# A mixture-of-experts kernel: the one-tile unit's second layer ahead of the next unit's transposes, and W1's low halves in two column halves

## The chip, the cores and the metric

The kernel runs on one core of a Trainium2 chip. The metric is the device time of one execution in microseconds. TensorE multiplies matrices, VectorE, ScalarE and GpSimd work elementwise, SyncE and GpSimd issue DMA transfers. Each engine runs its own instruction stream in order and waits for the others on semaphores.

## The reference

Attention with pooled keys and values, and then a routed two-layer network (8 experts) on the 4608 tokens that attention gives:

```python
k_p = k.reshape(B, H, Sp, 8, D).mean(axis=3); v_p = v.reshape(B, H, Sp, 8, D).mean(axis=3)
attn = softmax(scale * q @ k_p.T)                  # B = H = 8, 576 queries, 72 pooled keys, D = 64
x = (attn @ v_p).reshape(4608, 512)
do_compute = x @ w_skip > 0
xc = x[do_compute]
e_idx = argmax(xc @ w_gate);  gate_w = softmax(xc @ w_gate)[e_idx]
for e in range(8):                                 # w1[e]: 512 x 1024, w2[e]: 1024 x 512
    h = maximum(xc[e_idx == e] @ w1[e], 0.0)
    y[e_idx == e] = gate_w * (h @ w2[e])
out = x;  out[do_compute] = xc + y
```

All of it is float32. A product in the expert stage is made of three: each operand is split into a high half (rounded to the type that TensorE takes at full rate) and a low half (the rest), and high x high, low x high and high x low are added up in PSUM.

## The kernel before

**Stages.** The attention stage takes the first 150 us or so, writes x to the output and sorts the tokens by expert into a table. It also handles 256 tokens of the busiest expert ahead. What follows is the expert stage, `experts`, and the change lies there.

**Units.** Each expert's tokens are cut into tiles of 128. A unit is two tiles, an expert's last unit has three where the count of tiles is odd, and an expert with one tile has a unit of one. Places are 0, 1, 2: three tiles fill all, two fill 1 and 2, one fills 2 alone. The register `kind` says which it is: 0 is one tile, 1 two (`TWO` is 1), more than 1 three, and with three it also says how wide the first layer is, a step of `QUARTERS` by how full the last tile is. One and two tiles both run their first layer on columns 128 to 384. `ends` is 1 in an expert's last unit, 2 if its last tile has at most 64 tokens ("short"). `after` is the `ends` of the unit before. `left` counts the units still to come, this one with them.

**TensorE's order in a unit** (`unit` inside the tensor block): the first layer `first`, in eight blocks of 128 hidden columns `f`, 12 products each, with three PSUM tiles `psL` in turn. From `f` = 3 on it waits (`lo`) until VectorE is done with the block three before. Then `second(0)` and `second(1)` for the tiles in places 0 and 1, then `tx`, the transposes of the next unit's rows into `psD`, then the tile in place 2, as `second(2)` or, for a short tile, `second_short`. `tx` waits for `land0` to `land2`, which GpSimd gives once the gathered rows have landed. In a one-tile unit nothing stands between `first` and `tx`. `far_width` and `by_width` choose the body for the width with branches; TensorE's never had one for 352 and takes 384 there, ScalarE's and VectorE's did.

**ScalarE** makes the high half of each hidden block (`hhi`, ReLU). In an expert's first unit it makes the high halves of W2, one of four chunks at every second block; in an expert's last unit, behind the first layer, those of the next W1 (four chunks of 128 x 1024). Then it makes the high halves of the next x from `psD`, three tiles.

**VectorE** makes the low halves of the hidden blocks (`hlo`), of W2 and W1 (`split`), adds a second-layer result to its rows (`result`, `result_short`), and makes the low halves of x (`x_low`). Its order at the end of an expert is: four W1 splits, `result(0)` and `result(1)` where there are such tiles, `x_low` three times, which gives `x` and so lets TensorE's next `first` begin, then the result of place 2.

**Weight loads.** SyncE loads the weights in eight chunks of 512 KB an expert, strictly in order: four of W1, four of W2. A chunk's staging buffer is free once VectorE has split the chunk of the expert before (`wlo` counts the splits).

**GpSimd** scatters each finished tile to the output and gathers the rows of the unit after next into the freed ring buffer. It waits for a scatter's completion before it gathers into the same buffer, and only then for the landing of its gathers.

```python
with t.If(left > 1):
    tx(u)
with t.If(kind < TWO):
    for _ in range(3):
        P(t, "lo")
P(t, "psf0")
```

Of the kernel before, what the change touches and what calls it, by code (L numbers as in the profile page):

```python
# [26 lines left out]
F32 = mybir.dt.float32  # L27
# [4 lines left out]
ALU = mybir.AluOpType  # L32
# [9 lines left out]
NE, F = 8, 1024  # L42
# [20 lines left out]
TWO = 1  # L63
# [1 line left out]
PLACES = 2, 1, 0  # L65
SPARE = 10
BETWEEN = 5, 6, 7
QUARTERS = 288, 320, 352, 384
NEAR, FAR = 2, (0, 2, 1)
WARM, AGAIN = (24, 64), (39, 42)  # L70
FIRST = [b * S // 128 for b in range(B)]
# [18 lines left out]
def chunk_of(w, c):  # L90
    return w[0][:, c, :] if c < 4 else w[1][:, (c - 4) * 2:(c - 4) * 2 + 2, :]


def chunk_view(st, c):
    return st if c < 4 else st.rearrange("p (a n) -> p a n", a=2)
# [982 lines left out]
def experts(tc, nc, out, w1, w2, whi, wlo, slot, gate, nti, kinds_a, steps, lows, near, bufs, mb, ident, psum, upper):  # L1078
    stage = [bufs["stage"][:, i] for i in range(NST)]
# [4 lines left out]
    with tc.tile_critical(no_gpsimd_drain=True):  # L1084
        names = ("land0 land1 land2 gates pe act lo x l2 psf0 psf1 ob0 ob1 ob2 gat0 gat1 gat2 sc0 sc1 sc2 "
                 "whi wlo near go up down sum").split()
        sem = {n: nc.alloc_semaphore("m_" + n) for n in names + [f"wd{i}" for i in range(NST)]}

        def P(e, n, by=1):
            e.wait_ge(sem[n], by).then_inc(sem[n], -by)  # L1090
# [4 lines left out]
        @contextmanager  # L1095
        def when(e, cond, mark=None):

            name = f"when{nc.next_id()}"
            jump = e.br_cond(cond, name + "_then", name + "_past")
            if mark is not None:  # L1100
                jump.branch_hint(mark)
            with nc.body(name + "_then", valid_engines=[e.engine]):
                yield
                e.br(name + "_past")
            nc.switch_bb(name + "_past")
# [28 lines left out]
        def by_width(e, kind, go):  # L1134

            def three(lo, hi):
                if lo == hi:
                    return go(slice(0, QUARTERS[lo]))
                mid = (lo + hi) // 2
# [7 lines left out]
            with when(e, kind > TWO):  # L1147
                three(0, len(QUARTERS) - 1)

        def far_width(e, kind, go, marks):  # L1150

            name = f"wide{nc.next_id()}"
            widths = [slice(128, 384)] + [slice(0, n) for n in QUARTERS]
            jumps, froms = [], []
# [26 lines left out]
        with nc.Block(no_gpsimd_drain=True) as blk:  # L1181
# [79 lines left out]
            @blk.tensor  # L1261
            def _(t):
                at, turn = parity(t, 1)
                
                def tx(u):

                    o, after = at(), held[3]
                    t.reg_load(after, nti[0:1, bass.ds(u + 1, 1)])
                    three = t.snap(after, min_val=0, max_val=TWO + 4)
                    if LOOPED:  # L1270
                        for jump, mark in zip(jumps, widths_ahead(t, after)):
                            jump.branch_hint(mark)
                    for i in range(3):
                        P(t, f"land{i}")
                    for unit, this in ((0, o < 1), (1, o > 0)):
                        def place(i, n):
                            for k in range(4):
                                m = t.transpose(psD[i][:, k * 128:k * 128 + 128],
                                                ring[:, 3 * unit + i, k * 128:k * 128 + 128], ident)
                            m.then_inc(sem["pe"], n)  # L1280

                        with t.If(this):
                            with t.If(three > TWO):
                                place(0, 1)
                                place(1, 1)
                            with t.If(three < TWO + 1):
                                place(1, 2)
                            place(2, 1)
                    turn()

                def first(xs):

                    P(t, "x")
                    for f in range(8):
                        if f > 2:
                            P(t, "lo")
                        ps, w = psL[f % 3][:, xs], slice(f * 128, f * 128 + 128)
                        for k in range(4):
                            t.matmul(ps, whi[0][:, k, w], xhi[:, k, xs], start=(k == 0), stop=False)  # L1299
                            t.matmul(ps, whi[0][:, k, w], xlo[:, k, xs], start=False, stop=False)  # L1300
                            last = t.matmul(ps, wlo[0][:, k, w], xhi[:, k, xs], start=False, stop=(k == 3))  # L1301
                        last.then_inc(sem["pe"], 1)

                def second_short():

                    for k in range(8):
                        t.matmul(psF[0], hhi[:, k, 256:384], whi[1][:, k, :], start=(k == 0), stop=False)
                        last = t.matmul(psF[0], hhi[:, k, 256:384], wlo[1][:, k, :], start=False, stop=(k == 7))
                    last.then_inc(sem["down"], 1)

                def second(place, lo):

                    i = place % 2
                    if place < 2:
                        P(t, f"psf{i}")
                    sl, ps = slice(place * 128, place * 128 + 128), psF[i]
                    for k in range(8):
                        if lo and k in (4, 6):
                            for _ in range(k // 2 - 1):
                                P(t, "lo")  # L1320
                        t.matmul(ps, hhi[:, k, sl], whi[1][:, k, :], start=(k == 0), stop=False)  # L1321
                        t.matmul(ps, hhi[:, k, sl], wlo[1][:, k, :], start=False, stop=False)  # L1322
                        last = t.matmul(ps, hlo[:, k, sl], whi[1][:, k, :], start=False, stop=(k == 7))  # L1323
                    last.then_inc(sem["l2"], 1)

                def unit(u, kind, ends, _, left):
                    jumps[:] = far_width(t, kind, first, marks)
                    with t.If(kind > TWO):
                        second(0, True)
                        second(1, False)  # L1330
                    with t.If(kind < TWO + 1):
                        with t.If(kind > TWO - 1):
                            second(1, True)
                    with t.If(left > 1):
                        tx(u)
                    with t.If(kind < TWO):
                        for _ in range(3):
                            P(t, "lo")
                    P(t, "psf0")
                    with t.If(ends < 2):  # L1340
                        second(2, False)
                    with t.If(ends > 1):
                        second_short()

                assert len(steps) == SPARE
                steps[:6] = steps[2:6] + steps[:2]
                loads = registers(t, nti)
                held = next(loads)
                marks, jumps = [], []
                for n, (_, _, f) in enumerate(steps):  # L1350
                    if n == 5:
                        P(t, "lo")
                    i = int(not 4 <= n < 6)
                    m = f(psF[1 - i])
                    if m:
                        m.then_inc(sem["l2"], 1)
                    next(loads, None)
                    if n == 3:
                        marks = widths_ahead(t, held[1])
                    if n in BETWEEN:  # L1360
                        i = PLACES[BETWEEN.index(n)]
                        P(t, f"land{i}")
                        for k in range(4):
                            m = t.transpose(psD[i][:, k * 128:k * 128 + 128], ring[:, i, k * 128:k * 128 + 128], ident)
                        m.then_inc(sem["pe"], 1)
                units(t, held, unit)

            def half(f):
# [39 lines left out]
            def _(v):  # L1408
# [11 lines left out]
                    return v.tensor_tensor(xlo[:, :, sl], psD[i].rearrange("p (k n) -> p k n", k=4), xhi[:, :, sl].bitcast(F32),  # L1420
                                           ALU.subtract)

                def split(c):
                    P(v, "whi")
                    v.tensor_tensor(chunk_of(wlo, c), chunk_view(stage[c], c), chunk_of(whi, c).bitcast(F32),  # L1425
                                    ALU.subtract).then_inc(sem["wlo"], 1)

                def result(place):
                    i = place % 2
# [16 lines left out]
                def unit(u, kind, ends, after, left, load):  # L1446
# [31 lines left out]
                    with v.If(left > 1):  # L1478
                        with v.If(ends > 0):
                            for c in range(4):  # L1480
                                split(c)
                    with v.If(kind > TWO):
                        result(0)
                    with v.If(kind > TWO - 1):
# [1 line left out]
                    with v.If(left > 1):  # L1486
                        for i in range(3):
                            m = x_low(i)
                        m.then_inc(sem["x"], 1)
                    load()  # L1490
                    with v.If(ends < 2):
                        result(2)
# [8 lines left out]
                early(0)  # L1501
                for i in PLACES:
                    m = x_low(i)
                m.then_inc(sem["x"], 1)
                early(1)
                units(v, held, unit, True)
        nc.clear_and_free_semaphores(list(sem.values()))
# [57 lines left out]
```

## Time and profile before

| | |
|---|---|
| Time, median of 3 runs | 503.22 us (502.87 to 503.78) |
| Profiled execution | 501.07 us |
| Its span, first to last instruction | 499.3 us |
| TensorE busy | 476.4 us, 95% |
| VectorE, ScalarE, GpSimd busy | 292.8, 232.2, 213.3 us |
| Bytes moved by DMA | 87.11 MB, mean 174 GB/s |
| First-layer products (L1299 to L1301) | 3 x 384, 112.5 us each group |

Busy times are counted from one execution taken by the hardware profiler. The times of the runs come from other executions, so the two are near each other, not equal. TensorE's matmuls are pipelined: the duration shown for one is longer than the distance to the next, and the rate of a stretch is read from the starts.

### The profile page before, as it was taken

How to read it: one execution, taken by the hardware profiler on the slowest of the kernel's cores; microseconds unless marked ns; L12 is line 12 of the kernel's file. 1: busy time of each engine (PE TensorE's matmuls, PEld its weight loads, DVE VectorE, ACT ScalarE, POOL GpSimd, SP SyncE). 2: the span in 40 equal slices, each digit the busy share in tenths (PEclk: the TensorE clock that was granted, in tenths of full speed). 3: DMA queues.
4: the chain of work that ended last, by engine and by line, in shares of the span. 5: the costliest groups of instructions: out<-in, count | busy, mean ns of one | idle time of the engine just before them, and what ended most of it. 6: DMA issues, size and time to landing. Idle time of an engine off the chain costs nothing. (4 is left out here: it accounts for less than half of the span.)

```text
span 499.3 us, 10691 instructions
## 1 busy us (share of the span) xinstructions
PE 476.4 (95%) x3288; PEld 436.2 (87%) x3289; DVE 292.8 (59%) x745; ACT 232.2 (47%) x584; POOL 213.3 (43%) x273
## 2 busy tenths in 40 slices
PE   7999899999999997999999997999999999999994
PEld 6899899898989787898989897989899898989893
DVE  4877988888698435276665758633556553322321
ACT  5668679897881024163634446512345241212110
POOL 3489369789885321242314023522032223323221
PEclk9999999999999999999999998999999999999998
DMA  8999899975511176547463628641415110201101
GB/s 257 372 385 384 321 346 394 348 255 192 192 65 45 42 250 233 182 155 254 167 232 106 204 109 276 233 133 62 178 51 192 51 62 21 63 21 60 42 1 40
DMA packets 35414, 87.11 MB, mean 174 GB/s; under 512 B 7167, under 2 KB 9599, under 8 KB 33585
## 3 DMA queue, kind: packets, MB, share of 16 engines
q1 hardware_dynamic: 27536, 71.68, 40.8%
q0 software_dynamic: 7840, 14.99, 8.9%
q8 instruction: 16, 0.26, 0.2%
q14 instruction: 22, 0.17, 0.1%
HBM read 73.31 MB, written 20.71 MB: 188 GB/s over the span
## 5 line engine op out<-in xcount | busy, mean ns | idle before, releaser
L1299 PE MATMUL psl<-xhi,w1hi 128*128 128x256 f32 (+3 forms) x384 | 112.5, 293 | 0.3 <-PEq L1090 0.3
L1300 PE MATMUL psl<-xlo,w1hi 128*128 128x256 f32 (+3 forms) x384 | 112.4, 293 | 0.0
L1301 PE MATMUL psl<-xhi,w1lo 128*128 128x256 f32 (+3 forms) x384 | 112.4, 293 | 0.0
L1212 POOL DMA_INDIRECT out<-ring,slot x36 | 37.8, 1049 | 160.4 <-POOLq L1090 145.4
L1390 ACT ACTIVATE hhi<-psl 128x256 fp32r<-128x256 f32 (+3 forms) x96 | 39.3, 409 | 114.9 <-ACTq L1090 109.8
L1448 DVE SCALAR_TENSOR_TENSOR hlo<-psl,hhi 128x256 fp32r<-128x256 f32 (+2 forms) x96 | 40.4, 422 | 60.5 <-DVEq L1090 58.7
L1299 PEld LDWEIGHTS psl<-xhi,w1hi 128*128 128x128 f32 x384 | 72.1, 188 | 1.1 <-issue 0.7
L1300 PEld LDWEIGHTS psl<-xlo,w1hi 128*128 128x128 f32 x384 | 72.2, 188 | 0.4
L1301 PEld LDWEIGHTS psl<-xhi,w1lo 128*128 128x128 f32 x384 | 72.1, 188 | 0.0
L287 ACT ACTIVATE e<-sc,mn 128x72 f32<-128x72 f32 x288 | 64.9, 344 | 13.3 <-DVE mn L281 13.1
L1380 ACT ACTIVATE xhi<-psd 128x512 fp32r<-128x512 f32 x36 | 19.1, 598 | 74.4 <-ACTq L1090 74.4
L1207 POOL DMA_INDIRECT ring<-out,slot x39 | 43.0, 1103 | 22.3 <-issue 18.2
L312 PE MATMUL o<-vbd,pT 128*128 128x148 f32 (+1 forms) x312 | 49.3, 298 | 2.6 <-DVE x L334 1.5
L312 PEld LDWEIGHTS o<-vbd,pT 128*128 128x128 f32 (+1 forms) x312 | 38.5, 179 | 5.5 <-ACT pT L299 1.6
L1321 PE MATMUL psf<-w2hi,hhi 128*128 128x512 f32 x96 | 38.1, 396 | 2.9 <-PEq L1090 2.9
L1425 DVE TENSOR_TENSOR w2lo<-stage,w2hi 128x1024 fp32r<-128x1024 f32 x28 | 34.3, 1227 | 10.3 <-DVEq L1090 10.3
L397 POOL DMA_INDIRECT table<-pay,r_di x33 | 32.9, 998 | 15.2 <-DVE p_mx L421 7.5
L1322 PE MATMUL psf<-w2lo,hhi 128*128 128x512 f32 x96 | 37.4, 390 | 0.0
L1323 PE MATMUL psf<-w2hi,hlo 128*128 128x512 f32 x96 | 37.4, 390 | 0.0
L1322 PE MATMUL mb<-w2lo,hhi 128*128 128x512 f32 x88 | 34.3, 390 | 0.0
L1321 PE MATMUL mb<-w2hi,hhi 128*128 128x512 f32 x88 | 34.3, 390 | 0.0
L1323 PE MATMUL mb<-w2hi,hlo 128*128 128x512 f32 x88 | 34.3, 389 | 0.0
(254 smaller groups left out, 966.1 us busy)
## 6 DMA issues: line engine op xcount, KB each, us to landing
stage<-in_w SPq DMA_DIRECT2D x64, 512.0 KB, 3.4
out<-x SPq DMA_DIRECT2D x36, 256.0 KB
stage<-in_k SPq DMA_DIRECT2D x7, 1152.0 KB
qt<-in_q SPq DMA_DIRECT2D x9, 512.0 KB
hhi<-in_vm SPq DMA_DIRECT2D x4, 1024.0 KB
hlo<-in_vm SPq DMA_DIRECT2D x3, 1024.0 KB
xhi<-in_q SPq DMA_DIRECT2D x4, 512.0 KB
xlo<-in_q SPq DMA_DIRECT2D x4, 512.0 KB
```

The lines of the kernel that those rows point to most:

```text
L287: nc.scalar.activation(ev[:, h // 2, k0:k0 + SP], sc[:, h * SP:(h + 1) * SP], AF.Exp, bias=mn[:, 4 * i + h:4 * i + h + 1], scale=-1.0)
L312: nc.tensor.matmul(o_[sl, g * 2 * VA:(g + 1) * 2 * VA], pT[:, 2 * a + g, sl], vbd[b % 2][:, 2 * a + g, :], start=(g == 0), stop=False)
L1207: g.indirect_dma_start(ring[:, s % 6, 0:D], None, out, bass.IndirectOffsetOnAxis(ap=slot[:, s:s + 1], axis=0), bounds_check=NTOK - 1, oob_ ...
L1212: g.indirect_dma_start(out, bass.IndirectOffsetOnAxis(ap=offsets, axis=0), ring[:, s % 6, 0:D], None, bounds_check=NTOK - 1, oob_is_err=Fa ...
L1299: t.matmul(ps, whi[0][:, k, w], xhi[:, k, xs], start=(k == 0), stop=False)
L1300: t.matmul(ps, whi[0][:, k, w], xlo[:, k, xs], start=False, stop=False)
L1301: last = t.matmul(ps, wlo[0][:, k, w], xhi[:, k, xs], start=False, stop=(k == 3))
L1321: t.matmul(ps, hhi[:, k, sl], whi[1][:, k, :], start=(k == 0), stop=False)
L1322: t.matmul(ps, hhi[:, k, sl], wlo[1][:, k, :], start=False, stop=False)
L1323: last = t.matmul(ps, hlo[:, k, sl], whi[1][:, k, :], start=False, stop=(k == 7))
L1390: a.activation(hhi[:, f, xs], psL[f % 3][:, xs], AF.Relu).then_inc(sem["act"], 1)
L1448: return v.scalar_tensor_tensor(out[:, f, :], psL[f % 3][:, xs], 0.0, hhi[:, f, xs].bitcast(F32), ALU.max, ALU.subtract)
```

## The change

1. A one-tile unit runs its second layer right behind its first, waiting for the low halves of the hidden blocks in mid-stream (ahead of the fifth and the seventh pair), and the next unit's transposes come behind it. Other units keep their order.
2. VectorE splits the four W1 chunks in two halves of 512 columns: the first halves where the splits stood, the second halves behind the low halves of x. `x` is given twice, once behind x's low halves, once behind the second halves, and TensorE waits for it ahead of blocks 0 and 4.
3. The width 352 goes from `QUARTERS`: such units run at 384.

```diff
-QUARTERS = 288, 320, 352, 384
+QUARTERS = 288, 320, 384
...
                 def first(xs):
-                    P(t, "x")
                     for f in range(8):
+                        if f % 4 == 0:
+                            P(t, "x")
                         if f > 2:
                             P(t, "lo")
...
+                def waited(k):
+                    if k in (4, 6):
+                        for _ in range(k // 2 - 1):
+                            P(t, "lo")
+
-                def second_short():
+                def second_short(lo):
                     for k in range(8):
+                        if lo:
+                            waited(k)
...
+                    def third(lo):
+                        P(t, "psf0")
+                        with t.If(ends < 2):
+                            second(2, lo)
+                        with t.If(ends > 1):
+                            second_short(lo)
+
+                    with t.If(kind < TWO):
+                        third(True)
                     with t.If(left > 1):
                         tx(u)
-                    with t.If(kind < TWO):
-                        for _ in range(3):
-                            P(t, "lo")
-                    P(t, "psf0")
-                    with t.If(ends < 2):
-                        second(2, False)
-                    with t.If(ends > 1):
-                        second_short()
+                    with t.If(kind > TWO - 1):
+                        third(False)
...
-                def split(c):
-                    P(v, "whi")
-                    v.tensor_tensor(chunk_of(wlo, c), chunk_view(stage[c], c), chunk_of(whi, c).bitcast(F32),
-                                    ALU.subtract).then_inc(sem["wlo"], 1)
+                def split(c, part=slice(None)):
+                    if part.start is None or part.start == 0:
+                        P(v, "whi")
+                    view = (lambda y: y[:, part]) if c < 4 else (lambda y: y)
+                    m = v.tensor_tensor(view(chunk_of(wlo, c)), view(chunk_view(stage[c], c)), view(chunk_of(whi, c)).bitcast(F32),
+                                        ALU.subtract)
+                    if part.stop is None or part.stop == F:
+                        m.then_inc(sem["wlo"], 1)
...
                             for c in range(4):
-                                split(c)
+                                split(c, slice(0, F // 2))
...
                         m.then_inc(sem["x"], 1)
+                        with v.If(ends > 0):
+                            for c in range(4):
+                                split(c, slice(F // 2, F))
+                        v.engine_nop().then_inc(sem["x"], 1)
                     load()
...
-                m.then_inc(sem["x"], 1)
+                m.then_inc(sem["x"], 2)
```

## Rows read from the trace of the kernel before

**Rows 1.** Waits of TensorE, 170 to 500 us: total us, times, longest.
```profile
PE psf L1321 <- PEq L1090: 2.9, 1, 2.9
PE psd L1278 <- PEq L1090: 2.7, 1, 2.7
```

**Rows 2.** Groups by form, whole span: count, busy us, mean ns, idle before.
```profile
L1299 PEld LDWEIGHTS psl<-xhi,w1hi 128*128 128x128 f32 x384 | 72.1, 188 | 1.1 <-issue 0.7
...
L1322 PE MATMUL mb<-w2lo,hhi 128*128 128x512 f32 x88 | 34.3, 390 | 0.0
...
L1299 PE MATMUL psl<-xhi,w1hi 128*128 128x384 f32 x32 | 10.8, 339 | 0.0
...
L1390 ACT ACTIVATE hhi<-psl 128x384 fp32r<-128x384 f32 x8 | 3.9, 491 | 9.1 <-ACTq L1090 7.5 <-issue 1.6
```

**Rows 3.** Timeline of TensorE, 303 to 314 us: start, duration, instruction, idle before.
```profile
304.32 0.28 PE L1301 MATMUL psl<-xhi,w1lo 128*128 128x256 f32 x1
307.26 1.96 PE L1278 MATMUL psd<-cfs,ring 128*128 128x128 f32 x8 [2.66 <-PEq L1090]
...
313.25 0.28 PE L1299 MATMUL psl<-xhi,w1hi 128*128 128x256 f32 x1
```

**Rows 4.** Timeline of GpSimd, 290 to 335 us.
```profile
290.21 0.18 POOL L1206 COPY ring<-gate 128x1 f32<-128x1 f32 x1 [3.22 <-DMA out<-ring,slot]
...
299.77 0.67 POOL L1206 COPY ring<-gate 128x1 f32<-128x1 f32 x1 [1.89 <-DMA out<-ring,slot]
...
307.36 1.23 POOL L1212 DMA_INDIRECT out<-ring,slot  x1 [4.29 <-POOLq L1090]
...
329.13 1.02 POOL L1212 DMA_INDIRECT out<-ring,slot  x1 [4.98 <-POOLq L1090]
```

**Rows 5.** Windows: busy us of each engine, granted clock, DMA share, GB/s.
```profile
307.00:308.00 1.00, 0.74 (x4) 0.76 (x5) 1.00 (x2) 1.00 (x2) 0.64 (x1) 0.50 0.61 143
```

**Rows 6.** Timeline of TensorE one unit earlier, 288 to 294 us.
```profile
288.45 0.39 PE L1323 MATMUL mb<-w2hi,hlo 128*128 128x512 f32 x1
288.68 1.03 PE L1278 MATMUL psd<-cfs,ring 128*128 128x128 f32 x8
289.47 0.48 PE L1307 MATMUL psf<-w2hi,hhi 128*128 128x512 f32 x1
...
293.20 0.28 PE L1299 MATMUL psl<-xhi,w1hi 128*128 128x256 f32 x1
```

**Rows 7.** Timeline of ScalarE behind the one-tile unit's first layer.
```profile
305.24 3.91 ACT L1376 ACTIVATE w1hi<-stage 128x1024 fp32r<-128x1024 f32 x4
```

**Rows 8.** Timeline of VectorE, 306 to 319 us.
```profile
306.48 4.62 DVE L1425 TENSOR_TENSOR w1lo<-stage,w1hi 128x1024 fp32r<-128x1024 f32 x4
311.02 1.88 DVE L1420 TENSOR_TENSOR xlo<-psd,xhi 128x512 fp32r<-128x512 f32 x3
314.27 0.68 DVE L1439 TENSOR_TENSOR upper<-psf,upper 64x512 f32<-64x512 f32 x1 [1.37 <-DVEq L1090]
...
316.60 0.42 DVE L1448 SCALAR_TENSOR_TENSOR hlo<-psl,hhi 128x256 fp32r<-128x256 f32 x1 [0.57 <-DVEq L1090]
...
318.11 0.74 DVE L1448 SCALAR_TENSOR_TENSOR hlo<-psl,hhi 128x256 fp32r<-128x256 f32 x2
```

**Rows 9.** Timeline of TensorE, the next unit's fifth column block.
```profile
318.85 0.28 PE L1299 MATMUL psl<-xhi,w1hi 128*128 128x256 f32 x1
```

**Rows 10.** Timeline of VectorE at the expert end before, 290 to 295 us.
```profile
290.15 1.89 DVE L1420 TENSOR_TENSOR xlo<-psd,xhi 128x512 fp32r<-128x512 f32 x3 [0.19 <-DVEq L1090]
294.22 0.68 DVE L1439 TENSOR_TENSOR upper<-psf,upper 64x512 f32<-64x512 f32 x1 [2.18 <-DVEq L1090]
```

**Rows 11.** Windows of 2 us, columns as in rows 5.
```profile
296.00:298.00 2.00, 2.00 (x20) 2.00 (x19) 1.28 (x3) 1.08 (x4) 1.00 (x1) 1.00 0.00 0
```

**Rows 12.** Timeline of TensorE, the transposes of the unit after.
```profile
329.91 1.47 PE L1278 MATMUL psd<-cfs,ring 128*128 128x128 f32 x12
```

**Rows 13.** DMA queues, 236 to 480 us: packets, MB, share of 16 engines.
```profile
q14 instruction: 3, 0.02, 0.0%
```

More of the change, by code (lines that the diff above doesn't have):

```diff
@@ L1317, in second @@
                     for k in range(8):
-                        if lo and k in (4, 6):
-                            for _ in range(k // 2 - 1):
-                                P(t, "lo")
+                        if lo:
+                            waited(k)
                         t.matmul(ps, hhi[:, k, sl], whi[1][:, k, :], start=(k == 0), stop=False)
@@ L1333, in unit @@
                             second(1, True)
+                    def third(lo):
[6 more added lines that the diff above has]
+                        third(True)
                     with t.If(left > 1):
                         tx(u)
-                    with t.If(kind < TWO):
-                        for _ in range(3):
-                            P(t, "lo")
-                    P(t, "psf0")
-                    with t.If(ends < 2):
-                        second(2, False)
-                    with t.If(ends > 1):
-                        second_short()
+                    with t.If(kind > TWO - 1):
+                        third(False)
                 assert len(steps) == SPARE
```

## The prediction

> **What bounds the kernel now.** I read the waits of TensorE first, over the expert stage alone. The reader is to see how few there are: two idle stretches of 2.9 and 2.7 us [rows 1] in some 320 us. TensorE therefore sets the end, and only what shortens or lengthens its own stream, or one of these two stretches, moves the time. The first stands ahead of the second layer of the first unit (L1321) and nothing in the change touches that place. The second stands at the transposes (L1278) of one unit.
>
> The groups by form tell which unit. There are 11 units' worth of products into `mb` (88 at 8 a unit), while the first layer's 384 weight loads of one kind at 32 a unit make 12 units [rows 2]. So exactly one of twelve is a one-tile unit, and the part of the change that reorders TensorE acts once. The same view shows that only one unit is 384 wide on TensorE (32 products) and that its ReLUs were 384 wide too (8) [rows 2]. TensorE never had a 352-wide body, and a unit of that width would have run 384 there and 352 on ScalarE. None did, so dropping 352 moves no work here.
>
> Then the timelines around that unit, engine by engine. TensorE's last first-layer product starts at 304.32 and fills 0.12. The transposes start only at 307.26, and the next unit's first layer at 313.25 [rows 3]. GpSimd's next scatter, which it issues once the rows have landed, starts at 307.36 [rows 4]: the idle ended with the landing. [...] The same transposes and short product took 293.20 - 288.68 = 4.52 a unit earlier [rows 6], here 313.25 - 307.26 = 5.99 [rows 3]: the clock cost 1.47.
>
> But TensorE was not alone there. ScalarE made W1's high halves until 305.24 + 3.91 = 309.15, and only then the next x [rows 7]. VectorE made W1's low halves from 306.48, four of 4.62 in all, and the low halves of x until 311.02 + 1.88 = 312.90 [rows 8]. Without the idle and the clock's loss TensorE would have stood at 312.90 anyway, 0.35 earlier than it started. That is the key to the case: two chains end within 0.35 us of each other.
>
> **The change, part by part.** *TensorE's order.* The short product (eight pairs) takes 293.20 - 289.47 = 3.73 and the eight transposes 0.79 [rows 6]. Put right behind the first layer, it runs from 304.44 to 308.17. Its waits for VectorE's last low half do not bite: that half ends just before the W1 splits at 306.48 [rows 8], and it is needed for the last two of eight pairs, at 304.44 + 6/8 x 3.73 = 307.24. The transposes then run 308.17 to 308.96; the rows have landed by then if the gathers stay where they are. The idle of 2.8 us goes, but only moves: what is late next is x.
>
> *The low halves of W1.* One of four takes 4.62/4 = 1.155, one 512 wide by x's low halves 1.88/3 = 0.63 [rows 8]. The fourth half cannot start before ScalarE's fourth split at 309.15. So x's low halves run from about 309.8 and end at 309.8 + 1.88 = 311.7, against 312.90. The next first layer may start at 311.85 in place of 313.25: 1.4 us earlier, after an idle stretch of 311.85 - 308.96 = 2.9 us.
>
> *What takes the 1.4 back.* Behind x VectorE now has the four second halves, 4 x 0.63 = 2.5, to 314.2. Its next step, the sum of the short tile, started at 314.27 before [rows 8]: no time is gained there. From it hang the low halves of the next unit's hidden layer, the first at 316.60 and the second inside the pair that starts at 318.11 [rows 8], ending near 318.5. With three PSUM tiles TensorE's fifth column block needs that second one. It started at 318.85 before [rows 9] and cannot start before 318.55 now. So of 1.4 us at most 0.3 is left, if the clock holds over the idle. If it falls, I price it by the same loss as before, 1.47: the fifth block comes at 311.85 + 5.6 (four blocks, 318.85 - 313.25) + 1.47 = 318.92, 0.07 late. Both can be: the 2.7 us idle went with a fall, the 2.9 us one in [rows 1] is in a part of the trace without one. I take -0.15.
>
> *The other six expert ends.* There TensorE has no idle, so an earlier x gains nothing. The second halves go behind x: in the end ahead of the one-tile unit from 290.15 + 1.89 = 292.04 to 294.55, while the short sum started at 294.22 [rows 10]. It is 0.3 late, and with it the next unit's first low halves, for which the fourth column block waits, due at 293.20 + 3 x 1.4 = 297.4. The one other end of this kind (short tile, then a 256-wide first layer) behaves alike. Bounds 0 and 0.3 each; I take 0.1 each.
>
> *The weight loads.* A half split frees W1's staging only when its second half is done, so SyncE issues the next expert's four W1 loads about 9 us later, from 292.7 in place of about 281. SyncE's queue is in order and the W2 loads stand behind them, but those wait for splits in the next first layer anyway. W1 is wanted at 305.24 [rows 7], some 11 us after the last of four issues: hidden, unless it lands on other transfers. It does. From 296 to 298 the DMA stood still [rows 11], and just there the scatter's completion came after 1.89 us; when loads were in flight such a wait was 3.22 [rows 4]. The gathers behind it start up to 1.3 us later. For the one-tile unit the rows then land between 307.3 and 308.6, against 308.17 wanted: 0 to 0.4. One unit on, rows landed at about 329.0 (scatter at 329.13 [rows 4]) and the transposes came at 329.91 [rows 12]: 0 to 0.4 again, straight on TensorE. Were gathers faster behind an emptier queue of W2 loads, nothing would be gained, since nothing waits for them. I take 0.1 for both together, nearest to the rows with 0.9 of slack.
>
> *Branches and code.* Each unit takes one more jump, over a block of some 80 instructions. Such a jump stands today between the second layer and the transposes, where the starts at 288.45 and 288.68 lie one product apart [rows 6]; the other bound is the 2.9 us idle at L1321 [rows 1], which no named engine's work ends. I take 0: between 236 and 480 us the only instruction packets are three on one queue [rows 13], so the loop's code stays where it is. [...]
>
> Sum: -0.15 + 2 x 0.1 + 0.1 = +0.15. The profiled execution took 501.07 with a span of 499.3, so its like would be 501.2. It lies 2.15 under the median of the timed runs, 503.22, whose own spread is 0.9; on the median the forecast is 503.3.
>
> **The rivals.** (a) *x alone decides:* the hidden layer's low halves come earlier than I think, for instance because VectorE's second halves or its 0.57 us before the first of them shrink, and the clock holds. Then the whole 1.4 us stays: 501.8. For it speaks that x is the only thing TensorE waits for by name; against it that the sum at 314.27 does not move in my working.
>
> (b) *Late gathers turn it slower:* the W1 loads stretch the scatter and the gathers behind it. Place: the transposes behind the short product and those at 329.91. Deciding point: rows landing after 308.2 and 329.9. Price: x 0.5 late (312.35), then the lower clock over the first layer, 312.35 + 5.6 + 1.47 = 319.4 against 318.85, +0.57; +0.4 at 329.91; +0.2 for the low halves: +1.2, or 504.4, and more where the gathers themselves are stretched too. For it: the 3.22 against 1.89; against it: 2 MB of loads are gone in some 7 us.
>
> [...]
>
> (d) *The order does not bite:* the one-tile unit's low halves are late and the short product waits in mid-stream. Up to 0.5; it ends within the forecast.
>
> **How the numbers follow.** A measurement of this kernel can tell about 0.2% from no change, 1.0 us. The forecast with (d), between -0.3 and +0.7, has a chance of 0.68 and lies within that. (a) has 0.10 and is faster. (b) has 0.15 and (c) 0.07, both slower: together 0.22. The range runs from 502.2 to 504.9: it takes in the forecast's bounds with the spread of the timed runs, and (b); it leaves out (a) and (c), 0.17.
>
> **What would show it.** In the changed profile the short product should follow the one-tile first layer without a gap, and TensorE's idle of some 2.9 us should stand between the transposes and the next first layer. The first layer should start near 311.9 and its fifth block near 318.6 to 318.9, on the clock of before. The W1 low halves should stand as 56 pieces of 512 columns, half of them behind x. The forecast is wrong if that idle is missing or over 4 us, if the transposes at either two-tile unit wait for landing, or if TensorE stands idle at an end where it did not.

## The result: 0.6% slower, and the profile after

The changed kernel took 505.46 us (median of 15 executions, 502.44 to 508.65), the kernel before 502.60 us beside it (15, 499.76 to 504.08). The ratio is 1.0062 [1.0040, 1.0084], some 2.9 us lost. The forecast was 503.3 with a range to 504.9, which is 0.15 over a kernel before at 503.22: it was wrong. The profiled execution took 504.55 us with a span of 502.8 us.

TensorE's waits over the expert stage (total us, times, longest), to be read beside [rows 1]:

```profile
PE psl L1300 <- PEq L1090: 2.8, 2, 2.5
PE psf L1329 <- PEq L1090: 2.4, 1, 2.4
PE psd L1278 <- PEq L1090: 1.5, 1, 1.5
```

The idle at the first unit's second layer (L1329, L1321 before) is still there. The 2.7 us at the transposes have become 1.5 there and 2.5 at the next first layer. The timeline lines of TensorE and GpSimd around the one-tile unit, whose first layer starts at 294.79 (start, duration, instruction, idle before):

```profile
298.61 1.01 POOL L1212 DMA_INDIRECT out<-ring,slot  x1 [5.13 <-POOLq L1090]
303.61 0.18 POOL L1206 COPY ring<-gate 128x1 f32<-128x1 f32 x1 [3.99 <-DMA out<-ring,slot]
306.10 0.28 PE L1302 MATMUL psl<-xhi,w1lo 128*128 128x256 f32 x1
306.22 0.39 PE L1316 MATMUL psf<-w2hi,hhi 128*128 128x512 f32 x1
309.63 0.39 PE L1317 MATMUL psf<-w2lo,hhi 128*128 128x512 f32 x1
311.51 0.54 PE L1278 MATMUL psd<-cfs,ring 128*128 128x128 f32 x3 [1.49 <-PEq L1090]
311.56 1.11 POOL L1212 DMA_INDIRECT out<-ring,slot  x1 [4.26 <-POOLq L1090]
315.06 0.36 PE L1300 MATMUL psl<-xhi,w1hi 128*128 128x256 f32 x1 [2.47 <-PEq L1090]
327.88 0.40 PE L1329 MATMUL mb<-w2hi,hhi 128*128 128x512 f32 x1
```

The short product does follow the first layer without a gap, and then the picture departs from the forecast. The transposes stand 1.49 idle behind the short product. The next first layer starts 315.06 - 294.79 = 20.27 behind this unit's first, against 313.25 - 293.20 = 20.05 before [rows 3, 6]. And that layer takes 327.88 - 315.06 = 12.82, where it took 324.45 - 313.25 = 11.20 before [rows 3], as this timeline line of the kernel before shows:

```profile
324.45 0.40 PE L1321 MATMUL mb<-w2hi,hhi 128*128 128x512 f32 x1
```

GpSimd shows a second difference: it waited 3.99 us for the scatter's completion, against 1.89 [rows 4].

VectorE and ScalarE there, timeline lines as above:

```profile
308.24 0.69 DVE L1438 TENSOR_TENSOR w1lo<-stage,w1hi 128x512 fp32r<-128x512 f32 x1
...
312.28 1.57 ACT L1391 ACTIVATE xhi<-psd 128x512 fp32r<-128x512 f32 x3 [1.34 <-ACTq L1090]
313.03 1.88 DVE L1431 TENSOR_TENSOR xlo<-psd,xhi 128x512 fp32r<-128x512 f32 x3 [1.25 <-DVEq L1090]
314.83 2.48 DVE L1438 TENSOR_TENSOR w1lo<-stage,w1hi 128x512 fp32r<-128x512 f32 x4
```

ScalarE waited 1.34 and VectorE 1.25 for the transposes: x hangs on them now and no longer on the W1 splits. From the transposes' start to the first layer it is 315.06 - 311.51 = 3.55 us.

Windows of 2 us: busy us of TensorE, its weight loads, VectorE, ScalarE and GpSimd, granted clock, DMA share, GB/s:

```profile
296.00:298.00 2.00, 2.00 (x20) 2.00 (x19) 1.39 (x3) 1.47 (x3) 0.00 (x0) 1.00 1.01 387
...
316.00:318.00 2.00, 2.00 (x12) 2.00 (x11) 1.92 (x4) 0.34 (x2) 1.00 (x1) 0.50 0.85 270
```

Where the DMA stood still before (0.00 [rows 11]) it is full (1.01), and the granted clock, at 1.00 in all of that layer before, falls to 0.50 within the first us of the next first layer (0.79 from 315 to 316 us, 0.50 from 316 to 318).

The profiled execution is 3.5 us longer than the one before: 0.22 up to the next first layer, 1.62 in that layer, and 1.6 in the first unit, whose second layer's first product to the next column (195.89 to 203.05, 7.16 against 5.56) lost the clock (0.57 from 196 to 200 us, 1.00 before) behind an idle that the change doesn't touch. The last isn't the change's: after_fill below, with the whole change in it, has 5.51 there, and before_fill, which is the kernel before up to that place, 7.15, with starts 0.43 us apart up to 197.95, as in the changed kernel under the lower clock, and 0.23 from 198.29 on.

### The profile page after: what moved, and what is told of

Its sections match the earlier page's. It is cut to its first block, busy times and chain, and to the rows that moved or that the text cites. A ratio compares the mean times of both kernels' runs of the same rounds, so it can differ in the third digit from the quotient of the medians.

```text
span 502.8 us, 10761 instructions
## 1 busy us (share of the span) xinstructions
PE 477.7 (95%) x3288; PEld 437.0 (87%) x3289; DVE 297.1 (59%) x773; ACT 232.6 (46%) x584; POOL 210.4 (42%) x273
## 5 line engine op out<-in xcount | busy, mean ns | idle before, releaser
L1438 DVE TENSOR_TENSOR w1lo<-stage,w1hi 128x512 fp32r<-128x512 f32 x56 | 36.8, 688 | 8.1 <-DVEq L1090 7.6
L1329 PE MATMUL psf<-w2hi,hhi 128*128 128x512 f32 x96 | 38.6, 402 | 2.4 <-PEq L1090 2.4
L1448 DVE SCALAR_TENSOR_TENSOR ring<-mb,ring 128x512 f32 x11 | 8.3, 750 | 46.8 <-DVEq L1090 46.8
L1329 PE MATMUL mb<-w2hi,hhi 128*128 128x512 f32 x88 | 34.3, 390 | 0.0
```

What stands on the lines that cost most here:

```text
L1438: m = v.tensor_tensor(view(chunk_of(wlo, c)), view(chunk_view(stage[c], c)), view(chunk_of(whi, c)).bitcast(F32), ALU.subtract)
```

## The experiments

Each was timed beside the kernel before, whose median was 501.80 (34 executions) beside halves_only, order_only, late_loads and halves_one, 500.88 (17) beside one_hoist, after_hoist, order_fill and one_hoist_fill, and 501.22 (34) beside the last four. What a run lost is taken against the median beside it, and each trace is of one execution. Each is told as its edit against the changed kernel unless another is named. Two theories stood against each other: the loads that move make the rows land late (theory L in the expectations), or the new order itself costs (rival O), through TensorE's own queue and its clock.

**halves_only**: TensorE's old order, the rest of the change kept.

```diff
-                    with t.If(kind < TWO):
-                        third(True)
                     with t.If(left > 1):
                         tx(u)
-                    with t.If(kind > TWO - 1):
-                        third(False)
+                    with t.If(kind < TWO):
+                        for _ in range(3):
+                            P(t, "lo")
+                    third(False)
```

> The W1 halves and the two x signals of the change, but TensorE's order of the kernel before (transposes first). Theory L (the late weight loads delay scatter, gathers and so the landing of the next unit's rows): in the one-tile unit the transposes start 16.2 to 17.0 us behind the start of its first layer, as in the changed kernel (16.7) and not as before (14.1); the next first layer starts some 21 us behind it in place of 20.05, and the time is 1.0 to 2.5 us over before. Rival O (the new order itself costs the time, by the idle it puts behind the transposes): transposes at 14.1, time within 0.5 us of before.

506.40 us (503.26 to 510.15, 12), ratio 1.0092 [1.0063, 1.0120]: 4.6 us lost, more than by the whole change, though the two intervals overlap. Timeline lines, the first layer's last product starting at 307.10:

```profile
299.66 1.00 POOL L1212 DMA_INDIRECT out<-ring,slot  x1 [5.12 <-POOLq L1090]
305.26 0.79 POOL L1206 COPY ring<-gate 128x1 f32<-128x1 f32 x1 [4.59 <-DMA out<-ring,slot]
314.74 1.96 PE L1278 MATMUL psd<-cfs,ring 128*128 128x128 f32 x8 [7.36 <-PEq L1090]
314.84 1.02 POOL L1212 DMA_INDIRECT out<-ring,slot  x1 [5.12 <-POOLq L1090]
```

TensorE is idle for 7.36 us and goes on as GpSimd does, when the rows have landed: 314.84 - 300.66 = 14.18 us behind the issued scatter, where it was 307.36 - (299.77 - 1.89) = 9.48 before [rows 4]. The late landing is the cost here, and it is larger than theory L had it: the transposes came 18.90 behind the start of the first layer, not 16.2 to 17.0.

**order_only**: the new order, with W1's low halves whole at the old place.

```diff
-                                split(c, slice(0, F // 2))
+                                split(c)
...
-                        with v.If(ends > 0):
-                            for c in range(4):
-                                split(c, slice(F // 2, F))
```

> The new order alone: short product ahead of the transposes, but W1 split whole where it was, so the staging is freed as early as before. Theory L: rows land in time, the transposes follow the short product at 14.5 to 15.2 us behind the start of the first layer, x is ready at 19.7 and the next first layer starts at 19.8 to 20.1; idle ahead of it some 4 us, with the lower clock in the first layer behind it in part of the runs: time 0 to 1.5 us over before, at least 1 us under the changed kernel. Rival O: 2 to 3 us over before, like the changed kernel.

503.70 us (501.81 to 505.19, 12), ratio 1.0034 [1.0014, 1.0054]: 1.9 us lost (0.7 to 2.7 by the interval) without any late load. Timeline lines and a window:

```profile
300.80 0.67 POOL L1206 COPY ring<-gate 128x1 f32<-128x1 f32 x1 [1.89 <-DMA out<-ring,slot]
307.37 0.22 DVE L1463 SCALAR_TENSOR_TENSOR hhi<-psl,hhi 128x64 fp32r<-128x64 f32 x1
308.65 1.02 POOL L1212 DMA_INDIRECT out<-ring,slot  x1 [4.55 <-POOLq L1090]
308.90 0.39 PE L1317 MATMUL psf<-w2lo,hhi 128*128 128x512 f32 x1
310.70 0.54 PE L1278 MATMUL psd<-cfs,ring 128*128 128x128 f32 x3 [1.41 <-PEq L1090]
314.25 0.36 PE L1300 MATMUL psl<-xhi,w1hi 128*128 128x256 f32 x1 [2.47 <-PEq L1090]
327.08 0.39 PE L1329 MATMUL mb<-w2hi,hhi 128*128 128x512 f32 x1
```

```profile
316.00:318.00 2.00, 2.00 (x11) 2.00 (x11) 0.71 (x2) 1.33 (x2) 0.81 (x1) 0.50 0.60 234
```

The rows had landed by 308.65, and the transposes still came 2.05 us later, 16.47 behind the start of the first layer and not at 14.5 to 15.2. What they waited for is on TensorE's own queue. VectorE's last step on the hidden layer ended at 307.59; only then can TensorE's stream pass the wait ahead of the seventh pair and reach what stands between the short product and the transposes in `tx`, the read of the next unit's kind into a register and the hints for the jumps (`branch_hint`, set from that kind). The runs with the hoist below bear this out. In two-tile units these lie under running products (last product 288.45, transposes 288.68 [rows 6]), and in the one-tile unit before they lay under the wait for the rows (transposes 307.26, GpSimd's next step 307.36 [rows 3, 4]). The next first layer starts 20.02 us behind this unit's (20.05 before): nothing is gained. It takes 327.08 - 314.25 = 12.83, with the lower clock in it (0.50 from 316 to 318 us).

**late_loads**: the kernel before, with the W1 staging released only behind x. Splits, order and all else stay, so only the loads move.

```diff
-                                split(c)
+                                split(c, False)          # no wlo
...
                         m.then_inc(sem["x"], 1)
+                        with v.If(ends > 0):
+                            v.engine_nop().then_inc(sem["wlo"], 4)
```

> The kernel before, with one thing moved: W1's staging is given free behind the low halves of x (where the changed kernel's second halves begin) in place of right behind each split. No split is halved and TensorE's order is the old one. Theory L: as in the run with the halves alone, transposes of the one-tile unit's turn at 16.2 to 17.0 us and 1.0 to 2.5 us over before. Rival V (VectorE's extra and later work costs the time, through the low halves of the hidden layer): transposes at 14.1, time within 0.5 us of before.

504.62 us (503.08 to 506.78, 11), ratio 1.0050 [1.0028, 1.0072]: 2.8 us lost by the time of the loads alone. Timeline lines, and a window of DMA:

```profile
302.29 0.18 POOL L1206 COPY ring<-gate 128x1 f32<-128x1 f32 x1 [3.67 <-DMA out<-ring,slot]
309.74 1.96 PE L1278 MATMUL psd<-cfs,ring 128*128 128x128 f32 x8 [4.41 <-PEq L1090]
309.85 1.73 POOL L1212 DMA_INDIRECT out<-ring,slot  x1 [3.54 <-POOLq L1090]
316.76 0.28 PE L1299 MATMUL psl<-xhi,w1hi 128*128 128x256 f32 x1
```

```profile
296.00:298.00 2.00, 2.00 (x19) 2.00 (x18) 1.25 (x4) 1.35 (x3) 0.39 (x1) 1.00 0.95 324
```

The landing is the bound again (idle 4.41 against 2.66 [rows 3]). The next first layer starts 22.82 behind this unit's (293.94), 2.77 later than before. That is as much as the medians differ by, and rival V, with the transposes at 14.1, is out: they came at 15.80.

**halves_one**: the halves only in the one-tile unit, whole splits in all others.

```diff
+                            with v.If(kind < TWO):
+                                for c in range(4):
+                                    split(c, slice(0, F // 2))
+                            with v.If(kind > TWO - 1):
+                                for c in range(4):
+                                    split(c)
```

> The changed kernel, but the halves only at the end of a one-tile unit; at the other six expert ends W1 is split whole, early. Theory L: loads early again ahead of the one-tile unit, so transposes at 14.5 to 15.2 us behind the start of its first layer, next first layer at 18.6 to 19.2, time -0.3 to +1.3 us to before (the spread is the clock behind the idle) and 2 us or so under the changed kernel. Rival O: still 2 to 3 us over before.

504.22 us (500.93 to 505.40, 12), ratio 1.0040 [1.0017, 1.0063]. Timeline line of TensorE, whose first layer starts at 293.97:

```profile
310.45 1.08 PE L1278 MATMUL psd<-cfs,ring 128*128 128x128 f32 x8 [1.43 <-PEq L1090]
```

The loads wanted in this unit are early again, and yet it stands where order_only does, and not where theory L had it: the transposes came 16.48, the next first layer 20.03 behind this unit's first. That layer took 13.57: its starts lie 0.21 us apart from 314.35 to 318.61, as in order_only at 0.50, and 0.12 from 318.97 on, so the clock was low from its first products on.

**one_hoist**: halves_one, with the read of the kind and the jump hints put behind the first layer, so that they are done when `tx` comes. **after_hoist**: the changed kernel with the same.

```diff
-                def tx(u):
+                def ahead(u):
...
+                    with t.If(left > 1):
+                        ahead(u)
```

> As the run with the halves at the one-tile unit's end alone, and TensorE reads the next unit's kind and sets its jump hints right behind each first layer, ahead of the second layer, in place of ahead of the transposes. Theory S (with the short product first, TensorE's sequencer is held by the waits in mid-stream until the last low half, and the read and the jumps in front of the transposes, hidden elsewhere, then stand in the open): transposes 14.9 to 15.4 us behind the start of the one-tile unit's first layer in place of 16.5, next first layer at 18.5 to 19.0 in place of 20.0, time 0.5 to 1.2 us under the run without it, so 0.5 to 1.5 over before as long as the lower clock still falls on the next first layer. Rival W (something on the data's way holds the transposes): still 16.5, same time as without it.

> The changed kernel with the read and the hints ahead of the second layer. Theory L (there the transposes wait for the rows to land): nothing is gained, transposes still at 16.5 to 17.5 us or later, time within 0.6 us of the changed kernel, 2.5 to 3.5 over before. If only the sequencer held them (theory S alone): transposes at 15 and a time 1 us or more under the changed kernel.

506.73 us (505.61 to 507.30, 6), ratio 1.0112 [1.0088, 1.0135], and 508.38 (505.73 to 510.39, 6), 1.0134 [1.0099, 1.0169]. In one_hoist a gain was expected and 5.9 us were lost. In after_hoist none was expected, and the 7.5 us lost are more than twice the 2.5 to 3.5 expected; its transposes came behind an idle of 2.52, 18.86 behind the start of the first layer. TensorE in one_hoist, timeline lines of the one-tile unit and of a two-tile unit:

```profile
224.65 0.28 PE L1306 MATMUL psl<-xhi,w1lo 128*128 128x256 f32 x1
225.16 0.47 PE L1333 MATMUL mb<-w2hi,hhi 128*128 128x512 f32 x1 [0.23 <-PEq L1090]
...
306.84 0.28 PE L1306 MATMUL psl<-xhi,w1lo 128*128 128x256 f32 x1
308.02 0.49 PE L1320 MATMUL psf<-w2hi,hhi 128*128 128x512 f32 x1 [0.90 <-PEq L1090]
311.53 0.39 PE L1321 MATMUL psf<-w2lo,hhi 128*128 128x512 f32 x1
311.76 0.49 PE L1282 MATMUL psd<-cfs,ring 128*128 128x128 f32 x3
```

The gap in front of the transposes is gone (0.23 from start to start) and stands in front of the second layer: 1.18 instead of 0.12 here, 0.51 in the two-tile unit. So the gap does belong to the read and the hints, and it was moved, not removed. The next first layer came 19.53 behind this unit's, half a us earlier than in halves_one. But four other two-tile units are each 0.4 to 0.5 longer than before, and in the first unit the idle ahead of the second layer grew too, from 2.4 to 3.9 us.

**order_fill**, **after_fill**, **one_fill** and **one_hoist_fill**: order_only, the changed kernel, halves_one and one_hoist, with ten (the last: eleven) products behind the one-tile unit's `tx` whose result nobody reads, to keep TensorE busy while it waits for x.

```diff
                         tx(u)
+                        with t.If(kind < TWO):
+                            for _ in range(10):
+                                t.matmul(psL[2], hhi[:, 0, 128:256], whi[1][:, 0, :], start=True, stop=True)
```

> As the run with the new order alone, with ten products of 512 columns (0.23 us each, results not used) behind the transposes of the one-tile unit's turn, where TensorE waited for x. Theory C (the order costs its time by the clock, which the idle behind the transposes lowers over the next first layer): the next first layer takes 11.2 to 11.4 us in place of 12.8, its start stays at 20.0 to 20.3, and the time falls by 1.0 to 1.6 us against the run without them, to within 0.7 us of before. Rival D (VectorE's later steps cost it, the clock little): same time as without them, within 0.4 us.

501.21 us (500.00 to 503.45, 12), ratio 1.0013 [0.9992, 1.0034]. Timeline lines of TensorE and a window:

```profile
308.51 1.08 PE L1278 MATMUL psd<-cfs,ring 128*128 128x128 f32 x8 [1.21 <-PEq L1090]
309.35 0.48 PE L1355 MATMUL psl<-w2hi,hhi 128*128 128x512 f32 x1
312.09 0.36 PE L1300 MATMUL psl<-xhi,w1hi 128*128 128x256 f32 x1 [0.17 <-PEq L1090]
323.48 0.40 PE L1329 MATMUL mb<-w2hi,hhi 128*128 128x512 f32 x1
```

```profile
316.00:318.00 2.00, 2.00 (x19) 2.00 (x19) 1.48 (x3) 1.30 (x2) 0.21 (x2) 1.00 0.26 62
```

The next first layer takes 323.48 - 312.09 = 11.39 with the granted clock at 1.00 (312 to 320 us; its starts lie 0.12 apart to its end), against 12.83: what it lost was the clock. In time the step is 1.0034 to 1.0013 with overlapping intervals, so the layer's length is the firmer reading, though of one execution each.

> The changed kernel with the ten unused products behind the transposes of the one-tile unit's turn (as in the run with the new order and the products). Theories C and L side by side: the clock's part goes, the late landing stays. Next first layer 11.2 to 11.6 us long, transposes still at 16.5 us or later and waiting for the landing in most executions, time 1.0 to 2.0 us under the changed kernel and 0.8 to 2.2 over before. Were it all the clock: within 0.7 us of before. Were it all the landing: as the changed kernel, 3 us over.

504.22 us (501.05 to 506.74, 11), ratio 1.0054 [1.0032, 1.0076]. A gain over the changed kernel was expected, and none beyond the intervals is seen. Timeline lines:

```profile
301.03 1.16 POOL L1206 COPY ring<-gate 128x1 f32<-128x1 f32 x1 [4.22 <-DMA out<-ring,slot]
310.92 1.96 PE L1278 MATMUL psd<-cfs,ring 128*128 128x128 f32 x8 [3.75 <-PEq L1090]
311.02 1.03 POOL L1212 DMA_INDIRECT out<-ring,slot  x1 [5.16 <-POOLq L1090]
312.52 0.78 PE L1355 MATMUL psl<-w2hi,hhi 128*128 128x512 f32 x1
316.58 0.28 PE L1300 MATMUL psl<-xhi,w1hi 128*128 128x256 f32 x1
```

In this execution the rows landed 311.02 - (301.03 - 4.22) = 14.21 us behind the issued scatter, and TensorE waited 3.75 for them, ahead of where the added products stand. They can't help there: the next first layer keeps the clock (starts 0.12 us apart) and takes 11.21, and still starts 24.60 behind this unit's.

> New order, halves at the one-tile unit's end alone, and the ten unused products. Neither late loads nor the lower clock. Theory: x hangs on the transposes there (they start 16.5 us in, held by TensorE's own sequencer, and x follows 3.55 behind), so the halves give nothing: next first layer at 19.9 to 20.2, time within 0.5 us of the run with the new order and the products, -0.3 to +0.9 to before. If the halves are worth what they were worked out at, x comes 1 us earlier: next first layer at 19.0 or sooner.

501.78 us (500.24 to 504.30, 12), ratio 1.0016 [0.9996, 1.0035], the same as order_fill: the halves bring nothing once x hangs on the transposes (next first layer 19.81 behind this unit's, 19.84 in order_fill). In this execution they even cost, for the next unit's low halves wait behind VectorE's second halves: the layer's fourth column block stands 0.63 idle (first line), and the layer takes 12.26 against 11.39 at the same clock (starts 0.12 us apart in both). One unit on, the late loads show as well, in timeline lines:

```profile
318.40 0.35 PE L1300 MATMUL psl<-xhi,w1hi 128*128 128x256 f32 x1 [0.63 <-PEq L1090]
...
323.17 1.26 POOL L1206 COPY ring<-gate 128x1 f32<-128x1 f32 x1 [3.98 <-DMA out<-ring,slot]
332.23 0.43 PE L1278 MATMUL psd<-cfs,ring 128*128 128x128 f32 x2 [1.00 <-PEq L1090]
332.81 1.02 POOL L1212 DMA_INDIRECT out<-ring,slot  x1 [4.71 <-POOLq L1090]
```

> Halves at the one-tile unit's end alone, early read and hints, and eleven unused products of 0.23 us behind the transposes of that unit's turn. Theories L, S and C together say that all three costs are gone: transposes at 15, next first layer at 18.5 to 19.0 and 11.2 to 11.8 us long (VectorE's low halves hold its fourth and fifth block), time -0.7 to +0.2 us to before. If one of them is wrong the time stays 1 us or more over before.

506.03 us (504.92 to 506.75, 6), ratio 1.0096 [1.0073, 1.0120]: the hoist's cost stands, and the products bring no more against one_hoist than the intervals allow for.

**before_fill**: the kernel before with twelve such products ahead of the one-tile unit's `tx`, into `psD[0]`.

> The kernel before with twelve unused products of 0.23 us between the one-tile unit's first layer and the transposes, where TensorE waited 2.7 us for the landing. Theory: the lower clock that followed there fell on transposes and short product, which x outlasted, so keeping it up gives 0 to 0.5 us and no more. If that clock loss (1.47 us) counted in full: 1.2 to 1.6 us under before.

500.89 us (498.94 to 503.71, 12), ratio 0.9991 [0.9971, 1.0011], no difference that can be told. Timeline lines of TensorE:

```profile
304.60 2.93 PE L1337 MATMUL psd<-w2hi,hhi 128*128 128x512 f32 x12
...
313.19 0.35 PE L1299 MATMUL psl<-xhi,w1hi 128*128 128x256 f32 x1 [1.14 <-PEq L1090]
```

The clock is kept (the short product's starts lie 0.23 us apart), and TensorE then waits 1.14 for x: the next first layer starts only 0.22 sooner behind this unit's than before (19.83). Even this 0.22 need not be the clock's: quarters_only below, where the clock did fall at that place (starts 0.43 us apart from 307.61 to 309.31), has 19.82. In the kernel before, the clock's loss of 1.47 (granted clock 0.50 from 307 to 308 us [rows 5]) lay beside the W1 splits.

**quarters_only**: the kernel before without 352.

```diff
-QUARTERS = 288, 320, 352, 384
+QUARTERS = 288, 320, 384
```

> The kernel before with the width 352 dropped and nothing else. No unit has it, so all that changes is ScalarE's and VectorE's code. Every theory: within 0.5 us of before. If the length of the code counts: 1 us or more either way, with the idle ahead of the first unit's second layer longer or shorter.

501.60 us (499.56 to 502.99, 12), ratio 0.9992 [0.9968, 1.0016]. The medians differ by 0.4 the other way, and no difference can be told.

## Why the prediction was wrong

**"The weight loads" was mis-sized.** The mechanism stood in the text: the half splits free W1's staging behind x, the loads fall on the scatter, and the rows come late. I took 0 to 0.4 for each of two units, 0.1 in all, from one completion wait of 3.22. The runs have 3.67 to 4.59 with the loads in flight, and the landing behind the issued scatter takes 11.2 (late_loads), 11.9 (the changed kernel), 14.2 (halves_only, after_fill) where it took 9.5. That is 1.7 to 4.7 later, not up to 1.3. Without late loads ahead of this unit halves_one has 8.6 and order_only 9.7. late_loads, which moves nothing else, loses 2.8 us. This is rival (b), whose first place and deciding point (308.2) were right and whose price of 1.2 was too small. Its second place, one unit on, shows no wait in the changed kernel's profile, and 1.00 in one_fill's. The term's "about 9 us later" was short by its own figures too: from about 281 to 292.7 it is 11.7.

**"TensorE's order" missed a stall.** I had the transposes at 308.17, right behind the short product. The wait for the last low half was priced as harmless, because the product itself doesn't lose by it. But behind it stood the read of the next kind and the hints, and these were left without cover: 1.2 to 1.4 us of idle (order_only and halves_one, where the rows had landed by 308.65 and 307.25, order_fill and one_fill). "Branches and code" took 0 from a place where the same instructions lie under a two-tile second layer [rows 6]. The number was right for that place and wrong for this one. I had named the work that hides the edit there, and didn't ask whether it is there in the one-tile unit.

**The clock had the wrong sign.** "What takes the 1.4 back" gave -0.15 for x earlier and a clock that may fall. x isn't earlier: by the new order the W1 splits no longer bound it, and the transposes do, 3.55 ahead of it. An idle of 2.5 us now stands ahead of the first layer, and the clock's loss (1.62 in the changed kernel, 1.63 in order_only) falls on products that nothing outlasts. Before it fell on the transposes and the short product, which x outlasted: before_fill, which keeps the clock there, shows 0.22 at most for it in its trace.

**The parts don't add up.** Halves alone cost 4.6, the order alone 1.9, both 2.9. Where the rows land late, the short product fills part of the wait, and the order wins back some of the loss that the halves cause: with the same landing (14.18 and 14.21) the next first layer comes at 25.62 in halves_only, where the short product stands behind the transposes, and at 24.60 in after_fill. Where they land in time, the order costs.

**Rival (c), code.** No run shows a cost of the longer code, for which (c) had 0.07. The idle at L1329 is no longer than before (2.4 against 2.9 [rows 1]), so no wait was added there, and the loss has other places. Between 236 and 480 us the changed kernel's trace has the same three instruction packets as before [rows 13]. Whether the loop's code stays where it is, as the prediction reads them, no run shows. The hoist runs lengthened this idle to 3.9 us and more, but there the read and the hints lie in it too.

**What was right.** One unit in twelve is reordered and its idle moves instead of going. The short product ran without a wait in mid-stream, so rival (d) is out. The other expert ends show no new idle in the changed kernel's profile (halves_only has one, 0.55 at the second unit's transposes); ahead of the one-tile unit the first layer took 11.43 against 11.24, within the 0.3 that bounded it. The low halves come as 56 pieces, and the step in `QUARTERS` brings nothing. The working by which VectorE's second halves take the gain back held too: where the clock was kept, in one_fill, the low halves behind them came late, and the fourth column block with them, by 0.8. In the changed kernel the lower clock hid this: its layer takes 12.82, order_only's without second halves 12.83.

**Still open.** How the 2.9 us of an average execution divide among landing and clock: the changed kernel ranges over 6.2 us and the kernel before over 4.3, and one profile is one draw from that, here the fourth fastest of the 15. In it the transposes came with the landing (311.51 and 311.56) and behind a gap as long as order_only's, so both causes fit it. What ends the idle ahead of the first unit's second layer stays open. No version ran measurably faster than the kernel before.

## What to carry to other kernels

A split that finishes later also releases its buffer later: follow the release to the transfers that it starts, and ask what transfer, waited for by an engine, they will now run beside: the rows landed 1.7 to 4.7 us later here. A wait put in mid-stream can stop not only the products behind it but also the register reads and jump hints that used to run ahead under them: 1.2 to 1.4 us of idle here. And an idle stretch has a price by its place: a clock that fell over work which another chain outlasted cost 0.22 us at most here, and the same fall ahead of a long first layer cost all of its 1.6.

## What the hardware showed that was not expected

GpSimd's wait for the completion of its scatters took 1.89 us where the DMA had been still when the last of them was issued [rows 4, 11], and 3.67, 3.98, 3.99, 4.22 and 4.59 us in the runs where weight loads had been moved onto it. The read of a register and the hints left TensorE idle for 1.2 to 1.4 us once nothing covered them: in order_only 310.70 - 307.59 = 3.1 us passed between VectorE's last step and the transposes, of which the four products left in the stream explain some 0.9 (an estimate, four of sixteen that take 3.73 [rows 6]).
